# A fused attention and routing kernel: batch 1's queries projected sooner, the first quotient in halves, 1e-6 added by VectorE

## The chip, the cores and the metric

The kernel runs on one core of one Trainium2 chip. The metric is the device time of that core in microseconds (us). In what follows PE is TensorE, DVE is VectorE, ACT is ScalarE, POOL is GpSimd and SP is SyncE. All data are 32-bit floats. A "record" is a line of the profiler for one instruction; every matmul of this kernel leaves two of them.

## The reference

Two blocks follow each other. The first is a linear attention with a polynomial sketch: each query and key of 32 numbers is projected by two small matrices to 8 and 8 numbers, and their 64 products are its features. The second is a mixture of eight experts whose weights come from eight rounds of Sinkhorn normalization.

```python
batch, n_heads, seq, head_dim = (4, 4, 1088, 32);  r = 8

def phi(x):
    a = np.einsum('rd,bhsd->bhsr', S1, x)
    b = np.einsum('rd,bhsd->bhsr', S2, x)
    return np.einsum('bhsi,bhsj->bhsij', a, b).reshape(*x.shape[:-1], r * r)
q_p, k_p = (phi(q), phi(k))
kv = np.einsum('bhsf,bhsd->bhfd', k_p, v)
z = np.sum(k_p, axis=2)
num = np.einsum('bhsf,bhfd->bhsd', q_p, kv)
den = np.einsum('bhsf,bhf->bhs', q_p, z)[..., None] + 1e-06
attn = num / den                                  # x: (4352, 128) after a transpose

logits = x @ w_gate;  logits = logits - logits.max();  P = np.exp(logits)
for _ in range(8):
    P /= P.sum(1, keepdims=True) + 1e-09
    P /= P.sum(0, keepdims=True) + 1e-09
    P *= N / E
for e in range(E):                                # E = 8, F = 1024
    out += P[:, e:e + 1] * (np.maximum(x @ w1[e], 0.0) @ w2[e])
```

## The kernel before

The experts' matmuls are nearly all of the work. They are cut into *steps*: a step multiplies one tile of x by one 128-column piece of w1 (the line `first`, L914), ACT applies the relu, and the products with w2 (L1099) follow eight steps later. The products are computed by Strassen-like forms, for which DVE forms sums and differences of the relu's results (L931, later L978). The generator `work` yields one step at a time, and `fill(n)` puts steps worth `n` between the pieces of the attention and of the routing, so that PE has something to do while DVE, ACT and the transfers prepare the next piece.

```python
def fill(n):
    owed[0] += n
    while owed[0] > 0.25:
        owed[0] -= next(work)           # a step of 256 columns counts 0.57, of 480 columns 1
```

Batch 0 is the only one whose quotients can be had early. They are made in three chunks of queries, (0, 512), (512, 800) and (800, 1088). `fractions(c, 1)` puts the denominators of chunk c in a PSUM bank and `fractions(c, 0)` the numerators. `divide` turns them into x, transposed:

```python
def divide(c):
    lo, hi = chunks[c]
    n = hi - lo
    nb = n // 32
    pn, pd = (queries.pop((0, c, "pn", m)) for m in range(2))
    rd = wk.tile([P, 512], F32, tag="rd", name="rd")
    nc.vector.transpose(out=rd[:, 0:n], in_=pd[:, 0:n])
    rc = wk.tile([P, 16], F32, tag="rc", name="rc")[:, 0:nb]
    nc.vector.tensor_scalar_add(rc, rd[:, 0:n].rearrange("p (b r) -> p b r", r=32)[:, :, 0], 1e-6)
    nc.vector.reciprocal(rc, rc)
    rd = wk.tile([P, 512], F32, tag="rd", name="rd")
    nc.vector.transpose(out=rd[:, 0:n].rearrange("p (b r) -> p b r", r=32),
                        in_=rc.unsqueeze(2).to_broadcast([P, nb, 32]))
    nc.vector.tensor_tensor(xT[:, lo:hi], pn[:, 0:n], rd[:, 0:n], op=Alu.mult)
```

The other batches take another way. `queries_ab(b)` projects the queries (L426) and sends them through DRAM, so that they come back repeated in `ph` and `rb`; `times(b, c)` multiplies these to the features; `tops(b, c)` makes numerators and denominators of a third of the queries with tokens on the partitions, and adds 1e-6 to the denominators by a matmul of ones with a small constant; `over(b, c)` divides and transposes, and `take_over` brings the result into x through DRAM.

```python
eps = consts.tile([P, 3, H], F32, name="eps")
nc.gpsimd.memset(eps, 1e-6 / P)
# [...]
def tops(b, c):
    # [...] 12 matmuls of 66 columns into pn (L462)
    for s in range(2):
        nc.tensor.matmul(pn[64 * s:64 * (s + 1), :, :, D], ones[:, 0:64], eps, start=False, stop=True,
                         tile_position=(0, 64 * s))                                # L466
def over(b, c):
    pn = queries.pop((b, c))
    rc = wk.tile([P, 16], F32, tag="rc", name="rc")[:, 0:12].rearrange("p (t h) -> p t h", h=H)
    nc.vector.reciprocal(rc, pn[:, :, :, D])
    # [...] multiply, transpose
```

The first part of the program, where no step can be had before batch 0's first chunk is divided (the order of calls is the order on PE and DVE, but for what the scheduler moves within it):

```python
    for part_ in range(3):
        keys_products(0, part_)          # DVE, L331
    keys_sums(0)                         # PE, L347
    for i in range(2):
        multiply(0, i)                   # DVE, L384
    keys_kept(0)                         # ACT, L362: the sums, from PSUM into kvz
    transpose_q(1)                       # DVE, L297
    transpose_q(0, chunks[0][1])
    fractions(0, 1)                      # PE, L392: needs multiply(0) and kvz
    queries_ab(1)                        # PE, L426: needs transpose_q(1)
    fractions(0, 0)
    query_products(1)                    # PE, L376
    # [...] transfers of queries_ab(1)'s results
    divide(0)
    # [...]
    for i in range(2):
        multiply(1, i)
    transpose_k(1)
    fill(1.25)
    fractions(1, 1)
    fractions(1, 0)
    fill(0.75)
    divide(1)
    keys_ab(1)                           # PE, L314
```

Of the kernel before, what the change touches and what calls it, by code (L numbers as in the profile page):

```python
# [50 lines left out]
def kernel(  # L51
# [92 lines left out]
    for i in range(2):  # L144
        kvs.append(consts.tile([P, 2, 2, D + 1], F32, name=f"kvs{i}"))
        nc.gpsimd.memset(kvs[i], 0.0)

    eps = consts.tile([P, 3, H], F32, name="eps")
    nc.gpsimd.memset(eps, 1e-6 / P)

    v_slots = []
    for i in range(2):
# [142 lines left out]
    def transpose_q(b, lo=0, hi=S):  # L295
        to = kT if b == 1 else qT
        nc.vector.transpose(out=to[:, lo:hi], in_=loaded["q", b].rearrange("p a d -> p (a d)")[:, lo:hi])  # L297
# [94 lines left out]
            nc.tensor.matmul(t[64 * i:64 * (i + 1), 0:n], kvz[:, m, i].rearrange("p h d -> p (h d)"),  # L392
                             phs[0][:, i, lo:hi], start=True, stop=True, tile_position=(0, 64 * i))

    def divide(c):


        lo, hi = chunks[c]
        n = hi - lo
        nb = n // 32  # L400
        pn, pd = (queries.pop((0, c, "pn", m)) for m in range(2))
        rd = wk.tile([P, 512], F32, tag="rd", name="rd")
        nc.vector.transpose(out=rd[:, 0:n], in_=pd[:, 0:n])
        rc = wk.tile([P, 16], F32, tag="rc", name="rc")[:, 0:nb]
        nc.vector.tensor_scalar_add(rc, rd[:, 0:n].rearrange("p (b r) -> p b r", r=32)[:, :, 0], 1e-6)
        nc.vector.reciprocal(rc, rc)
        rd = wk.tile([P, 512], F32, tag="rd", name="rd")
        nc.vector.transpose(out=rd[:, 0:n].rearrange("p (b r) -> p b r", r=32),
                            in_=rc.unsqueeze(2).to_broadcast([P, nb, 32]))
        nc.vector.tensor_tensor(xT[:, lo:hi], pn[:, 0:n], rd[:, 0:n], op=Alu.mult)  # L410

# [41 lines left out]
    def tops(b, c):  # L455

        pn = bank()[:, 0:3 * H * (D + 1)].rearrange("p (t h d) -> p t h d", t=3, h=H)
        ph = third(phs[b % 2], c)
        for t in range(3):
            for i in range(2):  # L460
                for s in range(2):
                    nc.tensor.matmul(pn[64 * s:64 * (s + 1), t, 2 * i:2 * i + 2].rearrange("p h d -> p (h d)"),  # L462
                                     ph[:, i, s, 64 * t:64 * (t + 1)], kvs[b % 2][:, i].rearrange("p h d -> p (h d)"),
                                     start=(t == 0 and i == 0), stop=False, tile_position=(0, 64 * s))
        for s in range(2):
            nc.tensor.matmul(pn[64 * s:64 * (s + 1), :, :, D], ones[:, 0:64], eps, start=False, stop=True,  # L466
                             tile_position=(0, 64 * s))
        queries[b, c] = pn

    turned = {}  # L470
# [1 line left out]
    def over(b, c):  # L472
        pn = queries.pop((b, c))
        rc = wk.tile([P, 16], F32, tag="rc", name="rc")[:, 0:12].rearrange("p (t h) -> p t h", h=H)
        nc.vector.reciprocal(rc, pn[:, :, :, D])
        xs = wk.tile([P, 512], F32, tag="rd", name="rd")[:, 0:384].rearrange("p (h t d) -> p h t d", h=H, t=3)
        nc.vector.tensor_tensor(xs.rearrange("p h t d -> p t h d"), pn[:, :, :, 0:D],
                                rc.unsqueeze(3).to_broadcast([P, 3, H, D]), op=Alu.mult)
        if c == 0:
            turned[b] = wk.tile([P, H, W9], F32, tag="xt", name="xt", bufs=1)  # L480
        nc.vector.transpose(out=turned[b][:, :, 96 * c:96 * (c + 1)].rearrange("p h (t s) -> p h t s", t=3), in_=xs)
# [25 lines left out]
    def attention(b):  # L507


        follows = b + 1 < B  # L510
        keys_sums(b)
        times(b, 0)
        yield 2.2 if b == 1 else 2
        keys_kept(b)
        times(b, 1)
        tops(b, 0)
        if b == 1:
            transpose_q(2)
        yield 1.4
        times(b, 2)  # L520
        over(b, 0)
        tops(b, 1)
        if b == 1:
            queries_ab(2)
            repeat_a(2)
        if follows:
            repeat_b(b + 1)
        yield 1.4
        over(b, 1)
        if b + 1 == B:  # L530
            take_over(b, 0, 192, nc.gpsimd)
        yield 1.4
        tops(b, 2)
        if follows:
            transpose_k(b + 1)
        if b + 2 < B:
            load_k(b + 2)
            load_v(b + 2)
        yield 1.4
        over(b, 2)  # L540
        if b + 1 < B:
            take_over(b, 0, W9, nc.gpsimd)
        else:
            take_over(b, 192, W9, nc.sync)
        if follows:
            yield 0.7
            keys_ab(b + 1)
            yield 0.7
            if b == 1:
                transpose_q(3)  # L550
            keys_products(b + 1, 0)
            yield 1.4
            keys_products(b + 1, 1)
            if b == 1:
                queries_ab(3)
                repeat_a(3)
            yield 1.4
            keys_products(b + 1, 2)
            yield 1.4
# [10 lines left out]

    def routing():

        yield 5
        for c in range(len(chunks)):
            logits(c)
        yield 1
        for c in range(len(chunks)):
            logits_turned()
        lg = lgp[:, :, 0:E]
        mx = sk.tile([P, 1], F32, tag="mx", name="mx")  # L580
        nc.vector.tensor_reduce(out=mx, in_=lg, axis=AX.XY, op=Alu.max)
        yield 3
        pm = bank()[:, 0:P]
        for s in range(2):
            nc.tensor.matmul(pm[64 * s:64 * (s + 1)], mx.to_broadcast([P, 64]), ident, start=True, stop=True,
                             tile_position=(0, 64 * s))
        nc.vector.reduce_max(mx, pm, axis=AX.X)
        nc.vector.tensor_scalar(mx, mx, -1.0, 64 * math.log(2.0), op0=Alu.mult, op1=Alu.add)
        pw = p2s[0]
        nc.scalar.activation(out=pw[:, :, 0:E], in_=lg, func=Act.Exp, bias=mx[:, 0:1])  # L590

        step = 1.5 * 2.0 ** (23 - 149 + 64)
        nc.vector.tensor_scalar(pw[:, :, 0:E], pw[:, :, 0:E], step, step, op0=Alu.add, op1=Alu.subtract)
        for it in range(ITERS):
            rs = sk.tile([P, SA], F32, tag="rs", name="rs")
            nc.vector.reduce_sum(rs, pw, axis=AX.X)  # L596
            nc.vector.reciprocal(rs, rs)
            p1 = p1s[it % 2]
            nc.vector.scalar_tensor_tensor(p1[:, 0:SA], rs.unsqueeze(2).to_broadcast([P, SA, E]), UP,
                                           pw[:, :, 0:E], op0=Alu.mult, op1=Alu.mult)  # L600
            cs = sk.tile([P, E], F32, tag="cs", name="cs")
            nc.vector.reduce_sum(cs, p1.rearrange("p g e -> p e g"), axis=AX.X)  # L602
            yield 4.25
            pc = bank()[:, 0:E]
            for s in range(2):
                nc.tensor.matmul(pc[64 * s:64 * (s + 1)], ones[:, 0:64], cs, start=True, stop=True,
                                 tile_position=(0, 64 * s))
            cr = sk.tile([P, E], F32, tag="cr", name="cr")
            nc.vector.reciprocal(cr, pc)
            last = it == ITERS - 1  # L610
            pw = lgp if last else p2s[(it + 1) % 2]
            nc.vector.scalar_tensor_tensor(pw[:, :, 0:E], cr.unsqueeze(1).to_broadcast([P, SA, E]),
                                           float(N) / E * (1.0 if last else UP), p1[:, 0:SA],
                                           op0=Alu.mult, op1=Alu.mult)

        nc.vector.transpose(out=lgT.rearrange("p a s -> p (a s)"), in_=lgp.rearrange("p a e -> p (a e)"))
        for b in (1, 0, 2, 3):
            nc.sync.dma_start(out=pT[:, b * S:(b + 1) * S],
                                                  in_=lgT[32 * b:32 * b + E].rearrange("p a s -> p (a s)"))
# [300 lines left out]
    def two(k):  # L920
# [3 lines left out]
        h, ts, (later_h, earlier_h, t13) = hs[k] = room_of(k)  # L924

        def step(c):
            f, t = 2 * q + c // 2, c % 2
            first(k, f, t * n, (t + 1) * n, h[c], k % 2)

        def less(out, a, b):  # L930
            nc.vector.tensor_tensor(out, a, b, op=Alu.subtract)  # L931
# [242 lines left out]
# [3 lines that stand above are left out]
            owed[0] -= next(work)  # L1177

    with tc.manual_schedule(engines={engines.DVE, engines.PE, engines.Activation}):
# [7 lines left out]
        for part_ in range(3):  # L1187
            keys_products(0, part_)
        keys_sums(0)
        for i in range(2):  # L1190
            multiply(0, i)
        keys_kept(0)
        transpose_q(1)
        transpose_q(0, chunks[0][1])
        fractions(0, 1)
        queries_ab(1)
        fractions(0, 0)
        query_products(1)
        repeat_a(1)
        repeat_b(1)  # L1200
        divide(0)
        load_q(2)
    with tc.manual_schedule(engines={engines.DVE, engines.PE}):
        for i in range(2):
            multiply(1, i)
        transpose_k(1)
        load_k(2)
        fill(1.25)
        fractions(1, 1)
        fractions(1, 0)  # L1210
        fill(0.75)
        divide(1)
        keys_ab(1)
        fill(0.75)
# [56 lines left out]
```

## Time and profile before

| | |
|---|---|
| time, median of three runs | 920.4 us (920.19 to 921.06) |
| span of the profiled execution | 918.0 us |
| PE busy in matmuls | 911.2 us, 7442 records |
| L914, the first product, xe or xT by w1 | 569.8 + 119.7 us busy |
| L1099, the second product | 256.1 + 233.9 + 114.2 + 76.0 us busy |
| DVE busy | 678.9 us |
| ACT busy | 421.6 us |
| POOL busy | 204.0 us |
| granted clock of PE | full in every slice |

Busy times of PE's groups overlap, as two matmuls run at a time, one in each half of the array's columns; so PE's share of busy time doesn't tell how near PE is to what it can do. What a stage loses is read from the times at which matmuls start.

### The profile page before, as it was taken

What the parts mean: (1) busy time and instruction counts of PE and PEld (TensorE: products, weight loads), DVE (VectorE), ACT (ScalarE), POOL (GpSimd) and SP (SyncE); (2) the same over time, 40 slices, a digit from 0 to 9 for tenths busy, and PEclk for the clock granted to TensorE, in tenths of its full rate; (3) what the DMA queues carried; (4) which work ended last, traced back from release to release, by engine and by line L of the source; (5) the groups of instructions that cost most, each with busy time, mean ns of one, the idle gap of its engine ahead of it and who ended that gap; (6) DMA issues with size and microseconds to landing.
All of it is one profiled execution on the core that took longest, in us unless ns stands there. A gap on an engine that the chain in (4) does not pass through costs nothing.

```text
span 918.0 us, 18893 instructions
## 1 busy us (share of the span) xinstructions
PE 911.2 (99%) x7442; PEld 637.4 (69%) x7442; DVE 678.9 (74%) x1173; ACT 421.6 (46%) x915; POOL 204.0 (22%) x212
## 2 busy tenths in 40 slices
PE   9999999999999999999999999999999999999997
PEld 6777544466666677777777777777777655556886
DVE  7678699888776798666975656956567976758665
ACT  3455555554444454444544444544445444445443
POOL 3121100175545421201210010110100243210220
PEclk9999999999999999999999999999999999999999
DMA  9994100213454535534364343454445456453640
GB/s 254 308 273 163 54 1 1 70 64 127 148 150 139 186 119 174 165 110 150 114 185 134 117 143 112 132 187 127 133 122 165 130 170 195 162 166 92 177 153 13
DMA packets 91305, 128.15 MB, mean 140 GB/s; under 512 B 25392, under 2 KB 69504, under 8 KB 86480
## 3 DMA queue, kind: packets, MB, share of 16 engines
q1 hardware_dynamic: 88384, 121.42, 42.7%
q0 software_dynamic: 1600, 5.36, 2.1%
q8 instruction: 58, 0.95, 0.4%
q10 hardware_dynamic: 1232, 0.16, 0.1%
q14 instruction: 31, 0.25, 0.1%
HBM read 107.88 MB, written 19.05 MB: 138 GB/s over the span
## 4 chain that ended last, share of the span: by engine, by line
PE 97%; DVE 2%; ACT 1%; issue 0%; POOL 0%; DVEq 0%; POOLq 0%
PE a L914 51%; PE s L1099 41%; PE a L347 1%; PE a L462 1%; PE a L114 1%; DVE hb L931 1%; PE a L314 0%; PE s L376 0%; PE a L426 0%; PE s L392 0%; DVE cs L602 0%; PE a L496 0%; PE a L392 0%; ACT hb L918 0%; DVE rs L596 0%
## 5 line engine op out<-in xcount | busy, mean ns | idle before, releaser
L914 PE MATMUL a<-xe,w 128*64 128x256 f32 (+1 forms) x2560 | 569.8, 470 | 0.0
L918 ACT ACTIVATE hb<-a 128x256 f32<-128x256 f32 (+4 forms) x408 | 195.0, 480 | 241.5 <-PE a L914 209.3
L914 PEld LDWEIGHTS a<-xe,w 128*64 128x64 f32 x2560 | 263.0, 137 | 50.8 <-issue 1.8
L918 ACT ACTIVATE hx<-a 128x256 f32<-128x256 f32 (+1 forms) x360 | 167.3, 465 | 213.5 <-PE a L914 191.6
L1099 PE MATMUL s<-hb,ws 128*64 128x256 f32 (+3 forms) x1312 | 256.1, 395 | 0.2 <-DVE hb L931 0.2
L1099 PE MATMUL s<-hx,ws 128*64 128x256 f32 x1280 | 233.9, 379 | 0.0
L978 DVE TENSOR_TENSOR hb<-hb 128x512 f32<-128x512 f32 (+1 forms) x204 | 133.5, 664 | 102.8 <-ACT hb L918 98.8
L978 DVE TENSOR_TENSOR hx<-hx 128x512 f32<-128x512 f32 (+1 forms) x204 | 149.8, 744 | 65.0 <-ACT hx L918 60.2
L1099 PEld LDWEIGHTS s<-hb,ws 128*64 128x64 f32 x1312 | 134.9, 137 | 87.8 <-issue 64.5
L678 POOL TENSOR_TENSOR xe<-xT,xe 128x768 f32<-128x768 f32 (+2 forms) x41 | 80.3, 1958 | 481.2 <-DMA xe<-pT 377.0
L1099 PEld LDWEIGHTS s<-hx,ws 128*64 128x64 f32 x1280 | 132.7, 137 | 71.6 <-issue 50.3
L914 PE MATMUL a<-xT,w 128*64 128x416 f32 (+3 forms) x512 | 119.7, 462 | 0.0
L1099 PE MATMUL s<-hb,w 128*64 128x256 f32 (+3 forms) x536 | 114.2, 408 | 0.0
L1099 PE MATMUL s<-hx,w 128*64 128x256 f32 x384 | 76.0, 379 | 0.0
L931 DVE TENSOR_TENSOR hb<-hb 128x416 f32<-128x416 f32 (+7 forms) x84 | 60.7, 723 | 18.0 <-ACT hb L918 14.0
L1099 PEld LDWEIGHTS s<-hb,w 128*64 128x64 f32 x536 | 54.1, 137 | 19.0 <-issue 6.5
L914 PEld LDWEIGHTS a<-xT,w 128*64 128x64 f32 x512 | 48.9, 137 | 25.5 <-issue 15.7
L242 POOL TENSOR_TENSOR ws<-w 128x256 f32<-128x256 f32 (+1 forms) x70 | 60.5, 899 | 8.1 <-DMA w<-in_moe_w_dram 5.2
L931 DVE TENSOR_TENSOR hx<-hx 128x256 f32<-128x256 f32 (+1 forms) x65 | 39.5, 612 | 24.0 <-ACT hx L918 22.8
L1099 PEld LDWEIGHTS s<-hx,w 128*64 128x64 f32 x384 | 40.8, 137 | 6.6
L978 DVE TENSOR_TENSOR pqg<-hb 128x512 f32<-128x512 f32 x68 | 40.5, 637 | 0.0
L978 DVE TENSOR_TENSOR pqg<-hx 128x512 f32<-128x512 f32 x68 | 35.0, 554 | 0.0
(181 smaller groups left out, 485.0 us busy)
## 6 DMA issues: line engine op xcount, KB each, us to landing
w<-in_moe_w_dram SPq DMA_DIRECT2D x82, 512.0 KB, 5.5
ws<-ws SPq DMA_DIRECT2D x34, 1024.0 KB, 5.0
xe<-pT SPq DMA_DIRECT2D x34, 384.0 KB, 4.1
ws<-ws SPq DMA_DIRECT2D x12, 512.0 KB, 3.6
ph<-qa SPq DMA_DIRECT2D x12, 288.0 KB, 4.7
rb<-qb SPq DMA_DIRECT2D x3, 1152.0 KB, 7.2
pb<-pT SPq DMA_DIRECT2D x6, 384.0 KB, 8.3
kx<-in_k_dram SPq DMA_DIRECT2D x4, 544.0 KB, 4.0
```

The source lines that it names most:

```text
L114: nc.tensor.matmul(warm[:, 0:P], ones, ones, start=True, stop=True)
L242: tc.keep_in_program_order(nc.gpsimd.tensor_tensor(ws[:, c:c + len(ns)], blocks(x), blocks(y), op=Alu.subtract if off else Alu.add))
L347: nc.tensor.matmul(pv[64 * s:64 * (s + 1), i], kp[0:n, H * t + h].rearrange("p i j -> p (i j)"), vx[0:n, slots[h], t, :], start=(t == 0 an ...
L462: nc.tensor.matmul(pn[64 * s:64 * (s + 1), t, 2 * i:2 * i + 2].rearrange("p h d -> p (h d)"), ph[:, i, s, 64 * t:64 * (t + 1)], kvs[b % 2] ...
L678: tc.keep_in_program_order(nc.gpsimd.tensor_tensor(out, x, pb, op=Alu.mult))
L914: nc.tensor.matmul(ph[sl], loaded_w[j][0][:, P * f + H2 * s:P * f + H2 * (s + 1)], sources[j][:, lo:hi], start=True, stop=True, tile_posit ...
L918: nc.scalar.activation(out=out, in_=ph, func=Act.Relu)
L931: nc.vector.tensor_tensor(out, a, b, op=Alu.subtract)
L978: nc.vector.tensor_tensor(out if not isinstance(out, tuple) else places(*out), places(*a), places(*b) if isinstance(b, tuple) else b, op=A ...
L1099: nc.tensor.matmul(sums[g][i][H2 * s:H2 * (s + 1), n * place:n * (place + 1)], w, x, start=c == 1, stop=c == per, tile_position=(0, H2 * s))
```

## The change

It has five parts. (1) The queries of batch 1 are transposed and projected before `fractions(0, 1)`, where PE had waited for kvz. (2) The first quotient is made in two halves of 256 queries, and the first two blocks of steps are walked so that all four steps that need only the first 256 queries come first. (3) The 1e-6 of batches 1 to 3 is added by DVE and no longer by a matmul. (4) The larger piece of batch 3's x is sent by SP instead of POOL. (5) The numbers of steps ahead of numerators (`tops`), of fractions(1) and of the logits are larger, and some later ones smaller. The parts are meant to take waits and small matmuls off PE.

```diff
-    eps = consts.tile([P, 3, H], F32, name="eps")
-    nc.gpsimd.memset(eps, 1e-6 / P)
@@ divide
-    def divide(c):
+    def divide(c, parts=1):
-        n = hi - lo
+        n = (hi - lo) // parts
+        for i in range(0, hi - lo, n):
             # the same six operations, on pd[:, i:i + n], pn[:, i:i + n] and xT[:, lo + i:lo + i + n]
@@ tops
-                                     start=(t == 0 and i == 0), stop=False, tile_position=(0, 64 * s))
-        for s in range(2):
-            nc.tensor.matmul(pn[64 * s:64 * (s + 1), :, :, D], ones[:, 0:64], eps, start=False, stop=True,
-                             tile_position=(0, 64 * s))
+                                     start=(t == 0 and i == 0), stop=(t == 2 and i == 1), tile_position=(0, 64 * s))
@@ over
-        nc.vector.reciprocal(rc, pn[:, :, :, D])
+        nc.vector.tensor_scalar_add(rc, pn[:, :, :, D], 1e-6)
+        nc.vector.reciprocal(rc, rc)
@@ attention(b)
         keys_sums(b)
         times(b, 0)
-        yield 2.2 if b == 1 else 2
+        yield 2.8 if b == 1 else 2.5
         # [...]
         if b + 1 == B:
-            take_over(b, 0, 192, nc.gpsimd)
+            take_over(b, 0, 192, nc.sync)
         # [...]
-        yield 1.4
+        yield 1.4 if follows else 0.6
         over(b, 2)
@@ routing
-        yield 5
+        yield 6
         for c in range(len(chunks)):
             logits(c)
@@ two(k), the steps of a block of two tiles
         def step(c):
-            f, t = 2 * q + c // 2, c % 2
-            first(k, f, t * n, (t + 1) * n, h[c], k % 2)
+            b, f, t = k, c // 2, c % 2
+            if k < 2:
+                b, f, t = c // 2, c % 2, k
+            first(b, 2 * blocks[b][1] + f, t * n, (t + 1) * n, room_of(b)[0][2 * f + t], b % 2)
@@ the first part
         keys_sums(0)
+        transpose_q(1)
         for i in range(2):
             multiply(0, i)
         keys_kept(0)
-        transpose_q(1)
         transpose_q(0, chunks[0][1])
+        queries_ab(1)
         fractions(0, 1)
-        queries_ab(1)
         fractions(0, 0)
         query_products(1)
         # [...]
-        divide(0)
+        divide(0, 2)
         # [...]
-        fill(1.25)
+        fill(2.2)
         fractions(1, 1)
         fractions(1, 0)
-        fill(0.75)
+        fill(0.4)
         divide(1)
         keys_ab(1)
```

More of the change, by code (lines that the diff above doesn't have):

```diff
@@ L393, in fractions @@
                              phs[0][:, i, lo:hi], start=True, stop=True, tile_position=(0, 64 * i))
-    def divide(c):
+    def divide(c, parts=1):
         lo, hi = chunks[c]
-        n = hi - lo
+        n = (hi - lo) // parts
         nb = n // 32
         pn, pd = (queries.pop((0, c, "pn", m)) for m in range(2))
[L402 to L410, printed above, removed]
+        for i in range(0, hi - lo, n):
+            rd = wk.tile([P, 512], F32, tag="rd", name="rd")
+            nc.vector.transpose(out=rd[:, 0:n], in_=pd[:, i:i + n])
+            rc = wk.tile([P, 16], F32, tag="rc", name="rc")[:, 0:nb]
+            nc.vector.tensor_scalar_add(rc, rd[:, 0:n].rearrange("p (b r) -> p b r", r=32)[:, :, 0], 1e-6)
+            nc.vector.reciprocal(rc, rc)
+            rd = wk.tile([P, 512], F32, tag="rd", name="rd")
+            nc.vector.transpose(out=rd[:, 0:n].rearrange("p (b r) -> p b r", r=32),
+                                in_=rc.unsqueeze(2).to_broadcast([P, nb, 32]))
+            nc.vector.tensor_tensor(xT[:, lo + i:lo + i + n], pn[:, i:i + n], rd[:, 0:n], op=Alu.mult)
     def queries_ab(b):
@@ L474, in over @@
         rc = wk.tile([P, 16], F32, tag="rc", name="rc")[:, 0:12].rearrange("p (t h) -> p t h", h=H)
-        nc.vector.reciprocal(rc, pn[:, :, :, D])
+        nc.vector.tensor_scalar_add(rc, pn[:, :, :, D], 1e-6)
+        nc.vector.reciprocal(rc, rc)
         xs = wk.tile([P, 512], F32, tag="rd", name="rd")[:, 0:384].rearrange("p (h t d) -> p h t d", h=H, t=3)
```

## The prediction

> **What bounds the kernel now.** I read the page first, then the waits of PE, the chain, and the timeline of PE and DVE, stretch by stretch. The page:
>
> ```profile
> span 918.0 us, 18893 instructions
> ...
> PE 911.2 (99%) x7442; PEld 637.4 (69%) x7442; DVE 678.9 (74%) x1173; ACT 421.6 (46%) x915; POOL 204.0 (22%) x212
> ...
> PE 97%; DVE 2%; ACT 1%; issue 0%; POOL 0%; DVEq 0%; POOLq 0%
> ```
>
> PE carries the end: 97% of the chain. But busy time can't say how much is lost, so I counted columns. In the late, steady stage four steps with their products last 4.74 us by the chain; their columns at the rate of the timeline (two matmuls of 256 columns side by side every 0.43 us, which is 4 cycles of 2.4 GHz a column) come to 0.99 of that. Summed so over all 7442 records, the work is 890.1 us of the 918.0. Start times give where the other 28 lie: 4.4 us before 10 us (warm-up matmuls), 2.1 from 10 to 20, 5.9 from 20 to 100, 2.5 from 100 to 190, 7.7 spread evenly at 0.1 per 10 us, and 5.3 after the last matmul starts. The change touches only what lies from 10 to about 170 us, some 10 us of loss. That alone forbids a gain of 2% (18.4 us).
>
> The first part, on PE:
>
> ```profile
> 10.30 2.46 PE L347 MATMUL a<-v,kp 128*64 128x64 f32 x72
> 13.39 1.08 PE L392 MATMUL a<-ph,kvz 128*64 128x512 f32 x4 [0.63 <-ACT kvz L362]
> 14.30 1.15 PE L426 MATMUL a<-kT,wdq 128*64 128x192 f32 x12
> 15.28 1.03 PE L392 MATMUL a<-ph,kvz 128*64 128x512 f32 x4
> 16.24 1.24 PE L376 MATMUL s<-qT,wq 64*128 64x288 f32 x8
> 17.41 1.08 PE L914 MATMUL a<-xT,w 128*64 128x256 f32 x8
> 18.45 1.19 PE L392 MATMUL s<-ph,kvz 128*64 128x288 f32 x8
> 19.47 1.03 PE L914 MATMUL a<-xT,w 128*64 128x256 f32 x8
> 20.34 1.10 PE L314 MATMUL a<-wd,kT 128*64 128x64 f32 x32
> ```
>
> (start, duration, engine, line, out<-in, and in brackets an idle time and who ended it). There is one open wait, 0.63 us on ACT's copy to kvz. Some 0.1 us each is lost at 14.30, 17.41 (on the quotient) and 18.45 (on multiply(1)). DVE beside it:
>
> ```profile
> 12.14 1.30 DVE L297 STREAM_TRANSPOSE kT<-qx 128x1088 f32<-128x1088 f32 x1
> 13.36 0.73 DVE L297 STREAM_TRANSPOSE qT<-qx 128x576 f32<-128x576 f32 x1
> 14.55 0.72 DVE L403 STREAM_TRANSPOSE rd<-a 128x512 f32<-128x512 f32 x1 [0.46 <-PE a L392]
> ...
> 16.61 0.69 DVE L410 TENSOR_TENSOR xT<-a,rd 128x512 f32<-128x512 f32 x1
> 17.58 0.82 DVE L384 TENSOR_TENSOR ph<-ph,s 128x288 f32<-128x288 f32 x2 [0.28 <-PE s L376]
> ```
>
> DVE is never idle for long here: a divide of 512 lasts 2.75 us (14.55 to 17.30) and feeds PE at once. The small matmul that adds 1e-6, and a place in the routing where DVE's order costs PE time:
>
> ```profile
> 34.04 0.87 PE L462 MATMUL a<-kvs,ph 128*64 128x66 f32 x24
> 34.74 0.24 PE L466 MATMUL a<-eps,ones 128*64 128x12 f32 x4
> 34.83 0.63 PE L914 MATMUL a<-xT,w 128*64 128x256 f32 x4
> ```
>
> ```profile
> 161.82 0.95 DVE L931 TENSOR_TENSOR hb<-hb 128x768 f32<-128x768 f32 x1
> 162.69 0.20 DVE L609 RECIPROCAL cr<-a 128x8 f32<-128x8 f32 x1
> ...
> 164.79 0.66 DVE L602 TENSOR_REDUCE cs<-p 128x8 f32<-128x280 f32 x1
> 165.37 1.14 DVE L931 TENSOR_TENSOR hb<-hb 128x384 f32<-128x384 f32 x2
> ```
>
> **What the Trainium skill says.** "Perfetto Trace Analysis", section "Identifying the Most-Contended Engine", warns that the busy share of matmuls doesn't measure how near TensorE is to its limit; so it is here: 99% busy, 890 of 918 us of work. "TensorE: Matmul & The Clock Gate", "Back-to-back issue gap", gives matmuls of 1 to 64 columns a floor of about 60 cycles (25 ns): L466's four records of 12 columns occupy 34.74 to 34.83, 22 ns each, where their columns alone are worth 5. "VectorE: DVE Perf Modes", "The TRN2 errata", says that each instruction pays a fixed latency beside its elements: the transpose takes 0.72 us for 512 columns and 0.44 to 0.48 for 288 (L403 at 19.60 and 26.20), so a divide in halves costs more than one whole. "DMA: Bandwidth & Descriptors", "Issuing engines are not separate DMA queues", says that issuing from another engine saves only the issue: I expect nothing of part 4 by itself.
>
> **Part 3, 1e-6 by DVE.** Nine pairs of matmuls go (three batches by three thirds). Each occupies 0.087 us between the starts at 34.74 and 34.83; the other places give 0.06 to 0.09. 9 x 0.087 = 0.78 us, all on PE, which has no wait there: a gain of 0.75. DVE gets nine additions of 12 columns; the like of it (L405) lasts 0.17 and begins the next 0.21 later: 1.9 us of DVE between 36 and 100 us, where DVE idles 4.6 us before 32.8, 2.1 before 41.5 and 2.7 before 86.7. Off the path.
>
> **Parts 1 and 2, the first 25 us.** I lay the new order on the old durations. DVE: transpose of q(1) 10.94 to 12.24 (its load lands at 10.67, just in time), multiply(0) 12.16 to 13.43, transpose of q(0) to 14.09. PE: L347 is followed at 12.67 by queries_ab(1), 0.98 us, to 13.65; kvz is ready at 13.34, multiply(0) at 13.43, so the 0.63 wait is gone. Fractions(0, 1) to 14.52, fractions(0, 0) to 15.40, query_products(1) to 16.45. DVE begins to divide 1.16 after fractions(0, 1) begins, as before: 14.81. Half of it takes 0.46 + 0.21 + 0.26 + 0.52 + 0.42 = 1.87 (transpose, addition, reciprocal, transpose, product, by the spacing of the 288 chunk at 19.60, scaled to 256): 16.68, and PE starts steps at 16.78, after 0.33 of waiting. Four steps of 0.43 end at 18.51. The second half and multiply(1), which the built order interleaves, keep DVE until 18.7 (multiply(1)) and 19.05 (the last product); fractions(1) start at 18.74, a wait of 0.23, and end at 19.72; a fifth step to 20.16; keys_ab(1) waits 0.1 for transpose_k(1), 20.27. Before, keys_ab(1) began at 20.34 with four steps done. So the new order is ahead by a step, 0.43, and 0.07: 0.5 us. Of the 0.63 and the small losses a good half stays; DVE takes the rest. Queries of batch 1 leave 1.5 us sooner, and rb, which lands at 32.66 and is used at 32.79, comes sooner too; but PE did not wait for it.
>
> **Part 5, more steps ahead.** Before the numerators of the later batches PE loses a little, some 0.1 to 0.3 us at 62.6, 70.4, 87.4 and 96 by the start times, about 1 us together, part of it the change of shape that stays. I credit 0.2. The routing moves by three steps against the main work, so its DVE chains of 2.7 us (L609 to L602) fall elsewhere between the sums L931. Before, three of eight chains cut such a group in two, as above at 162.69 (others at 136.3 and 142.2), and PE waited at 139.64 (0.22), 145.51 (0.14) and 165.97 (0.35). In the built order of the changed kernel only two cuts by a chain remain, one at the maximum and exp (3.6 us long, with about 5.5 us until its sums are needed) and one at the last transpose (2.0 us). I credit 0.3 of the 0.7.
>
> **The sum.** 0.75 + 0.5 + 0.2 + 0.3 = 1.75 us. 920.4 - 1.75 = 918.65; I say 918.7.
>
> **The rivals.** (a) The routing ends too late. Counted in columns along the built order, its last sums stand at 156.5 us of work instead of 153.2, 3.3 later, while the first weighted step stands 1.4 later. Before, POOL began to weigh x at 179.98, when the transfer landed at 179.47; the first 512 columns of 768, two thirds of 3.02 us, are done at 182.0, and PE uses them at 184.21: 2.2 us to spare. The net delay is 3.3 - 1.4 = 1.9. That speaks for just no wait; and w2's load, which SP now issues ahead of the routing's result, must wait for PE's last product with the old w2, due at about 171.5, while the result is due at 172.8. If it fails, PE loses 0.5 to 1.5 us there: 919.5 to 920. (b) DVE becomes the bound of the first part: halves cost it 1 us more than one divide of 512, and if these durations are 0.1 longer each the four steps only fill a longer wait. The gain of 0.5 becomes 0: 919.2. (c) The waits only move: DVE's backlog in the routing lets PE wait at other sums. Then 0.3 turns into -0.7: 919.7. (d) All waits before numerators and in the routing go: another 1.2, 917.5. (e) Batch 3's x comes later, because SP issues the second piece's first transfer ahead of the first piece's loads. Landing at about 105.5, it is 3 us ahead of the logits, which move to about 108.5; a wait is unlikely.
>
> **Range and chances.** The parts are uncertain by 0.1, 0.4, 0.3 and 0.7, rival (a) adds up to 1, and the median by 0.3: 917.4 to 920.1 holds it 8 times in 10. All rivals together stay within 2 us, 2% is 18: same 0.98, faster 0.01, slower 0.01.
>
> **What would show it.** The idle time before L392 by kvz gone, and keys_ab(1) near 20.3 with five steps ahead of it; a wait of 0.2 to 0.4 before the first step, and one before fractions(1). No matmul of 12 columns, nine additions before the reciprocals, and PE straight from the numerators to the next step. POOL's first weighing no later than 182, no idle PE near 184, and fewer gaps before L1099 from 135 to 170. A stretch of PE idle over 1 us at 184, or transposes of 256 over 0.5 us, would make the prediction wrong.

## The result, and the profile after

The changed kernel takes 923.43 us (median; 922.18 to 924.35), the kernel before 920.39 (920.18 to 921.06): 1.003 times, 95% interval 1.0017 to 1.0043. The prediction said 918.7, 917.4 to 920.1. The change makes the kernel slower by about 3 us where a gain of 1.75 was forecast. The page of the changed kernel:

```profile
span 922.2 us, 18837 instructions
...
PE 910.9 (99%) x7406; PEld 566.3 (61%) x7406; DVE 694.0 (75%) x1187; ACT 420.4 (46%) x915; POOL 207.6 (23%) x206
...
PE 89%; DMA 5%; DVE 2%; POOL 2%; ACT 1%; issue 0%; SPq 0%; POOLq 0%; DVEq 0%; ACTq 0%
```

PE is as busy as before (910.9 for 911.2 us), with 18 matmuls (36 records) fewer. What tells more is the chain of work that ends last: PE holds 89% of it instead of 97%, and transfers (5%) and POOL (2%) have come in. It spends some 70 us more outside PE than before, 46 us of this between 240 and 320 us, where it goes round a loop of POOL and transfers. The waits of PE in the changed kernel (who was waited for, us in total, times, longest) show where it stands:

```profile
PE a L910 <- POOL xe L674: 1.5, 3, 0.5
PE a L424 <- DVE qT L294: 1.5, 1, 1.5
...
PE a L910 <- DVE rd L473: 0.6, 2, 0.3
PE a L460 <- DVE ph L451: 0.6, 1, 0.6
```

Before, this view named only the set-up wait for `own` (1.0), the 0.6 on kvz and a 0.2 in the routing. The 0.6 is gone, as predicted. New are the four shown, 0.5 for batch 1's keys, and two of 0.2.

The loss of PE, counted as in the prediction (start time less the columns' work of all records so far), in us by stretches of the span. E6 is an experiment below, the changed kernel without its attention yields:

| stretch, us | before | after | after less before | E6 |
|---|---|---|---|---|
| to 50 | 8.59 | 8.06 | -0.53 | 7.69 |
| 50 to 80 | 2.03 | 4.73 | +2.70 | 3.08 |
| 80 to 120 | 2.10 | 2.88 | +0.78 | 1.84 |
| 120 to 170 | 2.11 | 1.26 | -0.85 | 1.23 |
| 170 to 280 | 0.95 | 1.30 | +0.35 | 0.95 |
| 280 to 340 | 0.98 | 2.69 | +1.71 | 0.57 |
| 340 to 910 | 5.79 | 5.76 | -0.03 | 6.16 |

The stretches in which the prediction saw gains (the first 50 us, the routing from 120 to 170) did gain, 1.4 us together. Two stretches in which it expected next to nothing took 4.4: 50 to 80 and 280 to 340. (The two profiled executions are 4.2 us apart, spans of 922.2 and 918.0, where the medians are 3.0 apart; the table divides up the 4.2.)

**The wait at 54 us.** The changed kernel's timeline, PE, DVE and POOL, around the projection of batch 3's queries (start, duration, engine, line; idle time and its releaser in brackets):

```profile
50.27 2.90 DVE L930 TENSOR_TENSOR hb<-hb 128x576 f32<-128x576 f32 x1 [0.73 <-ACT hb L914]
50.45 0.74 POOL L201 TENSOR_TENSOR ws<-ws,w 128x256 f32<-128x256 f32 x1
...
51.83 0.72 POOL L203 TENSOR_TENSOR ws<-w,ws 128x256 f32<-128x256 f32 x1
53.10 1.30 DVE L294 STREAM_TRANSPOSE qT<-qx 128x1088 f32<-128x1088 f32 x1
54.54 0.87 PE L424 MATMUL a<-qT,wdq 128*64 128x192 f32 x8 [1.47 <-DVE qT L294]
```

One DVE sum that elsewhere takes 0.75 us lasts 2.90: it stands through POOL's three sums of weights. The transpose of the queries is behind it in DVE's queue, and PE waits 1.47 us for it. POOL's sums begin only now because POOL's queue is in order and its transfer of batch 1's x (L482) waits for that batch's last quotient; with more steps put ahead, the quotient ends at 49.5. Before, it ended at 45.9:

```profile
45.97 3.73 DVE L931 TENSOR_TENSOR hb<-hb 128x576 f32<-128x576 f32 x3
...
49.62 1.30 DVE L297 STREAM_TRANSPOSE qT<-qx 128x1088 f32<-128x1088 f32 x1
...
51.09 0.54 PE L426 MATMUL a<-qT,wdq 128*64 128x192 f32 x2
```

The same collision was there (three sums in 3.73 us), but the transpose ended at 50.92 and PE came for it at 51.09, 0.17 us later. The change brought no new collision. It used up 0.17 us of room.

**The waits from 68 to 73 us.** DVE's part of the changed kernel's timeline, with PE's waits:

```profile
64.49 0.46 DVE L737 TENSOR_TENSOR z<-x,z 128x288 f32<-128x288 f32 x1 [2.47 <-ACT x L746]
...
67.43 0.69 DVE L930 TENSOR_TENSOR hb<-hb 128x512 f32<-128x512 f32 x1 [1.31 <-ACT hb L914]
68.72 0.96 DVE L451 TENSOR_TENSOR ph<-ph,rb 128x768 f32<-128x768 f32 x1
69.82 0.92 PE L460 MATMUL a<-kvs,ph 128*64 128x66 f32 x24 [0.58 <-DVE ph L451]
```

DVE idles 2.47 us, 0.72 (between the lines) and 1.31 here and still makes PE wait. The profile shows nothing that the product `ph*rb` waits for itself, but it stands behind three operations of steps that were put ahead of it and that wait for ACT. Idle time in an in-order queue isn't room for what stands behind. The quotient that follows late, at 71.6, keeps a PSUM bank until its product `rd` is done, and PE waits 0.27 for that bank at 72.70, and 0.34 for another at 80.87.

**The waits from 282 to 322 us.** Here PE works through the experts in items. For each item POOL weighs x, that is, multiplies it by the tokens' routing weights (L674). POOL and the transfer queue of SP, in the changed kernel:

```profile
280.06 2.29 POOL L674 TENSOR_TENSOR xe<-xT,xe 128x768 f32<-128x768 f32 x1 [7.12 <-DMA xe<-pT]
...
292.19 0.33 SPq L243 DMA_DIRECT2D ws<-ws  x1
292.61 0.38 SPq L670 DMA_DIRECT2D xe<-pT  x1
299.75 2.28 POOL L674 TENSOR_TENSOR xe<-xT,xe 128x768 f32<-128x768 f32 x1 [7.59 <-DMA xe<-pT]
```

POOL weighs x, sums the weights of the next item (283.01 to 292.2), and SP stores these sums (L243). The next routing row (L670) stands behind that store in SP's queue, lands 7 us later, and only then can POOL weigh again. The loop takes 19.69 us here (280.06 to 299.75). Where PE waits for nothing, it needs 18.95 us for an item (before, four items from 222.31 to 298.12 us). Its 19.68 in the changed kernel (282.41 to 302.09) are the loop's pace, with half a us of waiting in each item.

The loop isn't always so slow. Its rounds from 241.64 us on last 19.07, 19.35, 19.69 and 19.74 us, those of E6 from 255.78 on 19.07, 19.00 and 18.57. In the rounds of 19.7 us POOL's own work has grown. In the changed kernel the weighing above, at 280.06, falls on sums of DVE that begin at the same time:

```profile
279.99 0.69 DVE L977 TENSOR_TENSOR hb<-hb 128x512 f32<-128x512 f32 x1 [2.31 <-ACT hb L914]
280.60 2.64 DVE L977 TENSOR_TENSOR pqg<-hb 128x512 f32<-128x512 f32 x2
```

In E6 it falls into the idle time of DVE ahead of the same sums:

```profile
274.85 1.82 POOL L674 TENSOR_TENSOR xe<-xT,xe 128x768 f32<-128x768 f32 x1 [7.41 <-DMA xe<-pT]
276.88 0.69 DVE L977 TENSOR_TENSOR hb<-hb 128x512 f32<-128x512 f32 x1 [2.31 <-ACT hb L914]
277.49 1.56 DVE L977 TENSOR_TENSOR pqg<-hb 128x512 f32<-128x512 f32 x2
```

The weighing takes 2.29 us for 1.82, and the ten sums of weights after it 9.15 for 8.57. Two things come together, then, and no run separates them: the loop has no room left (0.05 us from the end of a weighing to PE's use of it at 243.51; 1.09 before and 0.90 in E6 at the same item), and its own operations are longer. Little room alone doesn't make the loss. E10 below has 0.08 us of room at that item, but its next two rounds last 18.64 and 18.76 us, with sums of 8.95 and 8.76 us and a weighing of 1.82, and no such wait follows. Nor does the late first weighing by itself: it is at 184.64, 4.66 us later than before (179.98), but PE's first use of it is 3.87 us later as well (188.08 for 184.21).

### The profile page after: what moved, and what is told of

The parts are those of the page before. It is cut to its first block, busy times and chain, and to the rows that moved or that the text cites. A ratio compares the mean times of both kernels' runs of the same rounds, so it can differ in the third digit from the quotient of the medians.

```text
span 922.2 us, 18837 instructions
## 1 busy us (share of the span) xinstructions
PE 910.9 (99%) x7406; PEld 566.3 (61%) x7406; DVE 694.0 (75%) x1187; ACT 420.4 (46%) x915; POOL 207.6 (23%) x206
## 4 chain that ended last, share of the span: by engine, by line
PE 89%; DMA 5%; DVE 2%; POOL 2%; ACT 1%; issue 0%; SPq 0%; POOLq 0%; DVEq 0%; ACTq 0%
PE a L910 48%; PE s L1098 40%; DMA xe<-pT 2%; DMA kx<-in_k_dram 1%; POOL ws L239 1%; DMA w<-in_moe_w_dram 1%; DVE hb L930 1%; POOL xe L674 1%; PE a L344 1%; DMA v<-in_v_dram 1%; PE a L460 0%; DVE kT L299 0%; PE a L424 0%; PE a L311 0%; DVE ph L451 0%
## 5 line engine op out<-in xcount | busy, mean ns | idle before, releaser
L910 PE MATMUL a<-xe,w 128*64 128x256 f32 (+1 forms) x2560 | 532.5, 470 | 1.5 <-POOL xe L674 1.5
L910 PEld LDWEIGHTS a<-xe,w 128*64 128x64 f32 x2560 | 214.8, 137 | 86.2 <-POOL xe L674 2.9
L1098 PE MATMUL s<-hb,ws 128*64 128x256 f32 (+3 forms) x1312 | 237.9, 395 | 0.0
L1098 PE MATMUL s<-hx,ws 128*64 128x256 f32 x1280 | 213.6, 379 | 0.0
L977 DVE TENSOR_TENSOR hx<-hx 128x512 f32<-128x512 f32 (+1 forms) x204 | 156.2, 777 | 54.4 <-ACT hx L914 48.8
L674 POOL TENSOR_TENSOR xe<-xT,xe 128x768 f32<-128x768 f32 (+2 forms) x41 | 83.6, 2041 | 501.2 <-DMA xe<-pT 356.6
L1098 PEld LDWEIGHTS s<-hb,ws 128*64 128x64 f32 x1312 | 113.0, 137 | 101.0 <-issue 68.4
L1098 PEld LDWEIGHTS s<-hx,ws 128*64 128x64 f32 x1280 | 109.9, 137 | 93.1 <-issue 67.1
L1098 PE MATMUL s<-hb,w 128*64 128x256 f32 (+3 forms) x536 | 108.1, 408 | 0.0
L1098 PE MATMUL s<-hx,w 128*64 128x256 f32 x384 | 70.6, 379 | 0.0
L977 DVE TENSOR_TENSOR pqg<-hb 128x512 f32<-128x512 f32 x68 | 48.4, 752 | 0.0
```

The costliest lines, as they stand in the source:

```text
L674: tc.keep_in_program_order(nc.gpsimd.tensor_tensor(out, x, pb, op=Alu.mult))
L910: nc.tensor.matmul(ph[sl], loaded_w[j][0][:, P * f + H2 * s:P * f + H2 * (s + 1)], sources[j][:, lo:hi], start=True, stop=True, tile_posit ...
L977: nc.vector.tensor_tensor(out if not isinstance(out, tuple) else places(*out), places(*a), places(*b) if isinstance(b, tuple) else b, op=A ...
L1098: nc.tensor.matmul(sums[g][i][H2 * s:H2 * (s + 1), n * place:n * (place + 1)], w, x, start=c == 1, stop=c == per, tile_position=(0, H2 * s))
```

## Experiments on the change: undone, and each part alone

Times are medians with the ratio to the kernel before on the same chip (there 920.04 to 920.36 us) and its 95% interval. In the texts on record, theory A says that the added steps make the loss, B the first 25 us, C the 1e-6 on VectorE. Where the text subtracts the medians of two experiments, these can come from different chips. By the ratios, the change costs 2.8 us instead of 3.04, E1 gives back 2.3, E6 3.7 and E7 1.9 us, and E9 to E12 lie 1.7, 1.1, 1.5 and 0.6 us above E6: differences of a few tenths shouldn't be read.

**E1: all added steps taken back** from the changed kernel.

```diff
-        yield 2.8 if b == 1 else 2.5
+        yield 2.2 if b == 1 else 2
-        yield 1.4 if follows else 0.6
+        yield 1.4
-        yield 6      # routing
+        yield 5
```

> The changed kernel with the numbers of steps ahead of numerators, of the last quotient and of the logits as before (2.2 and 2, 1.4, 5); the rest of the change stays. Theory A, more steps ahead: they put sums that wait for later matmuls in front of batch b's products and quotients in DVE's queue, and start the routing, and with it POOL, later. Then the waits at 54.5 (1.5 us), 70 to 81 (1.2) and 282, 302, 322 (0.5 each) go, and the time is 918.5 to 919.5. Theory B, the first part (parts 1 and 2) shifts the phase of the steps: nothing comes back, 922 to 924. Theory C, the nine additions lengthen each quotient on DVE: also 922 to 924.

920.68 us, ratio 1.0005 (0.9996 to 1.0013): 2.75 us of the 3.04 come back, and none of the waits at 54, 68 to 73 and 282 to 322 us stands in its trace. Theory A, though 1.2 us above the upper end of what it expected.

**E2: only the added steps**, on the kernel before (the same three lines, the other way).

> The kernel before with only the larger numbers of steps ahead (2.8 and 2.5, 0.6 at the end of batch 3, 6 before the logits). Theory A: most of the loss is here, 923 to 925, with PE waiting for DVE at 54 and at 70 and for POOL near 280 to 320. Theories B and C: 920 to 921.

922.77 us, 1.0028 (1.0018 to 1.0039). A again, 0.2 below its range. Its trace has waits for the weighed tokens, 2.1 us in three at 261 to 320 us, but neither the one at 54 nor those at 68 to 73, which A had expected. So the added steps bring POOL's waits by themselves, and DVE's waits only together with the rest of the change; with which part of it wasn't separated.

**E3: only the first 25 us** (the new order, the halves, the fills), on the kernel before.

> The kernel before with only parts 1 and 2, the first 25 us (order, quotient in halves, walk of the first two blocks, fills of 2.2 and 0.4). Theory A: a gain of 0.4, 920.0. Theory B: the loss is here, 922 to 923, with the wait at 54 for DVE.

920.21 us, 1.0001 (0.9992 to 1.0009). Against B; of the predicted 0.5 nothing can be measured. The trace gives it and takes it: the loss at 24 us is 0.2 us lower than before, and at 35.5 PE waits 0.6 us for the first numerators, whose `rb` comes too late.

**E4: only the 1e-6 on VectorE**, on the kernel before.

> The kernel before with only part 3, 1e-6 added by DVE instead of by a matmul. Theory A: a gain of 0.75, 919.6. Theory C: the longer quotients make PE wait for banks and products, 921.5 to 923.

922.07 us, 1.0017 (1.0009 to 1.0025). A miss for A: this part alone is slower, within C's range. Of the waits that C names, the trace has one for a bank, 0.3 us. It puts most of the loss in another place, the logits:

```profile
108.08 1.26 PE L491 MATMUL a<-xT,wg 128*32 128x512 f32 x15 [0.97 <-DMA xT<-xd]
```

PE waits 0.97 us for batch 3's x, which goes through DRAM. In the kernel before, the second piece's store was issued at 98.58 and the read at 101.19; here 99.44 and 104.12. So 0.86 us of the delay is the quotient's, and 2.1 are the store's own time, which was 2.6 us before and 4.7 here. Whether each execution has that longer store is open: there is one trace.

## Experiments on the cause: which step, through which queue

**E5: only the routing's start back** (`yield 5`), in the changed kernel.

> The changed kernel with only the routing's head start put back from 6 steps to 5. Theory P (the three waits of 0.56 us for weighed tokens at 282 to 322 us stand because the routing ends later and GpSimd's loop, whose period is one item of work, never makes up for it): the waits there vanish, 1.7 us come back, and of the routing's small waits between 140 and 170 us about 1 us returns; 922.3 us (921.6 to 923.0). Rival Q (those waits come of slower GpSimd operations, not of a late start): they stay, and the time is 923.4 or above.

921.77 us, 1.0018 (1.001 to 1.0026). The first weighing moves from 184.64 to 182.40, the three POOL waits are gone, and the wait at 54 us is 1.5 us still. The 1.7 us come back as theory P says; the small waits of the routing, which it expected to return, do not. But POOL's operations are short again as well (weighings of 1.82 us from 258 us on, sums of 8.4 to 8.9), so this run doesn't rule out rival Q, that slower GpSimd operations make the waits.

**E6: only the attention's steps back** (the first two lines of E1), routing left at 6.

> The changed kernel with only the attention's head starts put back (2.2 and 2 steps for 2.8 and 2.5, and 1.4 for 0.6), the routing left at 6. Theory A (more steps put ahead on VectorE fill its queue, so that its products and transposes come late): the waits at 54, 70, 73 and 81 us go, 3.3 us; if the waits at 282 to 322 us stay, 920.1 us, and if they go as well, 918.5 us. Rival Q (a wait given up in one place is taken in another): at least half of it comes back before 120 us, 921.8 us or more.

919.08 us, 0.999 (0.9983 to 0.9997): faster than both kernels, 4.35 us below the changed one. In its waits nothing is left but the set-up's 1.0 us and one of 0.3 for a sum at 69.9 us, and the page's chain is PE's again:

```profile
PE 98%; DVE 1%; ACT 0%; issue 0%; POOL 0%; DVEq 0%; ACTq 0%; POOLq 0%
```

The POOL waits went too, although the routing still starts after 6 steps. The attention ends sooner; the first weighing (179.93) and PE's first use of it (182.98) come some 5 us sooner. Both new groups of waits hang on the attention's yields. Rival Q fails: its loss at 120 us is 12.61, the changed kernel's 15.67.

**E7: batch 3's queries transposed sooner.** The changed kernel, all yields as in the change:

```diff
         over(b, 2)
+        if b == 1:
+            transpose_q(3)
...
-            if b == 1:
-                transpose_q(3)
             keys_products(b + 1, 0)
```

> The changed kernel with batch 3's queries transposed right after batch 1's last quotient, ahead of the step's sums, so that GpSimd's sums no longer stand between. Theory A1 (the wait of 1.5 us at 54 us is one VectorE sum stretched from 0.75 to 2.90 us while GpSimd adds, with the transpose queued behind it): the wait goes and nothing else moves, 921.8 us (921.2 to 922.4). Rival Q (the delay only passes to the next reader of VectorE's results within 20 us): 923.0 us or more, with a new wait between 54 and 75 us.

920.88 us, 1.0009 (1.0002 to 1.0016). One line moved gives back 2.5 us. In its trace the sum is stretched all the same (POOL adds from 50.07 to 52.17), but nothing that PE needs soon stands behind it:

```profile
49.08 1.27 DVE L294 STREAM_TRANSPOSE qT<-qx 128x1088 f32<-128x1088 f32 x1
...
50.28 2.52 DVE L930 TENSOR_TENSOR hb<-hb 128x576 f32<-128x576 f32 x1
```

A1 holds for the wait: it is gone, and the ones at 67.8, 70.6 and 78.8 us keep their 0.59, 0.26 and 0.34. The rest of the gain I had not expected: the POOL waits vanish too. The first weighing is 2.28 us sooner (182.36), but PE's first use of it is 2.06 us sooner as well (186.02), so the loop has won little on PE: 0.40 us of room at 241.4 instead of 0.05. From 258 us on its weighings take 1.82 us again. The two losses don't add, but neither is simply the cause of the other: E2 has POOL's waits without the wait at 54 us, and E5 the wait at 54 us without POOL's.

**E8: the loop opened.** The changed kernel, with the store out of SP's queue:

```diff
-        nc.sync.dma_start(out=stored_four[e], in_=ws)
+        nc.gpsimd.dma_start(out=stored_four[e], in_=ws)
```

> The changed kernel with the sums of four blocks stored through GpSimd's own queue instead of SyncE's, so that SyncE's next load of a routing row no longer stands behind that store. Theory P (GpSimd's loop of load, weighing, sums and store is closed through SyncE's queue, and its period of 19.7 us is above the item's 19.0): the loop opens, the three waits at 282 to 322 us vanish, 921.7 us (921.2 to 922.3). Rival Q (GpSimd waits for a buffer that TensorE frees, or for the landing alone): the waits stay, 923.4 us.

921.70 us, 1.0031 (1.0016 to 1.0046). Five runs, two of them at 923.8 and 924.7, so that median and ratio differ and the gain is uncertain; the trace is clear. The waits at 282 to 322 us are gone, and the loss at 340 us is 18.66 for 20.92. Its trace:

```profile
276.66 7.99 POOL L239 TENSOR_TENSOR ws<-w 128x256 f32<-128x256 f32 x10 [8.01 <-PE a L910]
281.47 0.33 SPq L670 DMA_DIRECT2D xe<-pT  x1
...
285.56 1.83 POOL L674 TENSOR_TENSOR xe<-xT,xe 128x768 f32<-128x768 f32 x1
```

The row is fetched while POOL still sums (281.47), the weighing follows the sums with no idle time, and from 243 us on it is done 10 to 13 us ahead of PE. The first weighing was as late as in the changed kernel (184.5): with the loop open the late start brings no wait for POOL, and theory P holds against the Q of this run (a buffer, or the landing alone).

## Experiments on what each part is worth without the bad yields

All four are compared with E6 (919.08 us, ratio 0.999). They ran on another chip, where the kernel before takes 920.04 us instead of 920.29; measured from it, the differences from E6 are 0.25 us larger than those of the medians.

**E9: E6 with the last quotient after 0.6 steps again** (the changed kernel with only the first yield put back).

> The changed kernel with only the first of the two attention yields put back (2.2 and 2 steps for 2.8 and 2.5); the last quotient of batch 3 still comes after 0.6 steps. Theory A (the added steps ahead of the first numerators, in batches 1 and 2, make all the waits between 54 and 81 us): none of them stands, and the time is that of the kernel with both put back, 919.1 us (918.6 to 919.7). Rival R (the shortened last quotient carries part of the loss, by the wait of 0.37 us at 116 us and what follows it): 919.8 us or more.

921.01 us, 1.0009 (1.0001 to 1.0016): 1.9 us more than E6. Of the changed kernel's waits between 54 and 81 us none stands in its trace, and none for POOL: as theory A says, it is the yield ahead of the first numerators that makes them. The time is rival R's, but not by the wait at 116 us that I named, which isn't there. The trace has two other places:

```profile
108.19 0.67 PEld L492 LDWEIGHTS a<-xT,wg 128*32 128x32 f32 x15 [0.68 <-DMA xT<-xd]
161.39 0.54 PE L1098 MATMUL s<-hb,ws 128*64 128x384 f32 x1 [0.43 <-DVE hb L930]
```

Six routing steps count from the attention's end; ending it 0.8 steps sooner puts the logits at 107.36 instead of 108.61, and they meet the landing of batch 3's x. E1 has 5 steps after 1.4, one routing step fewer, and waits in the same two places (0.63 at 108.3, 0.62 of loss at 161.6) at 920.68. E1 less E6 is what the sixth step buys, 1.6 us; E9 less E6 is what the shortened yield costs, 1.9: one cancels the other.

**E10: E6 with the matrix products for the 1e-6 again.**

> The kernel with both attention yields put back, and besides with the 1e-6 added by the matrix products on TensorE again. By the prediction's step (24 small products gone are worth 0.75 us when no wait takes their place) it is 0.75 us slower than with them gone: 919.8 us. Rival C (VectorE's longer quotient costs as much as TensorE saves, as the part alone on the kernel before had it, 1.7 us slower): it is equal or faster, 919.1 us or less.

919.69 us, 1.0002 (0.9993 to 1.0011): 0.6 us slower by the medians, the intervals overlap. (The 24 products of the text are 18, in 36 records.) It agrees with the predicted 0.75, but it isn't clean: in its trace `rb` lands about 1.1 us later than in E6 (its product starts at 34.18 for 33.10), and PE waits 0.89 us there.

**E11: E6 with the first 25 us as before.**

> The kernel with both attention yields put back, and besides with the first 25 us as before (batch 1's queries after the products, the first quotient whole, the old order of steps and fills). By the prediction's step the first part is worth 0.5 us: 919.6 us. Rival C (worth nothing, as alone on the kernel before, or passed on to the wait for batch 1's keys at 20 us): 919.1 us.

920.74 us, 1.0006 (0.9998 to 1.0014): 1.7 us slower by the medians, where 0.5 was expected. At 50 us its loss is 1.03 us above E6's (8.72 for 7.69); the 0.63 for kvz is back among it. Another 0.61 stands at 160.7 us, where PE waits for a sum that DVE has late.

**E12: E6 with batch 3's first piece sent by GpSimd again.**

> The kernel with both attention yields put back, and besides with the first two thirds of batch 3's x sent by GpSimd again and not by SyncE. By the prediction's step this moves no wait by itself: 919.1 us. Rival S (the landing of batch 3's x is what the logits wait for, as in the kernel with the 1e-6 alone, where TensorE stood 1.25 us for it at 108 us): a wait of the logits for that transfer of 0.5 to 1.5 us stands near 107 us, 919.6 to 920.6 us.

919.53 us, 0.9996 (0.9988 to 1.0003), the profiled span 916.7 for 917.0. It can't be told from E6, and no wait for the transfer stands near the logits: rival S fails here.

## Why the prediction was wrong, point by point

- **The step that failed: "Part 5, more steps ahead", and in it "I credit 0.2"** for the later numerators. I asked only which small waits of PE more steps could fill. The steps also put their sums into DVE's queue ahead of what PE needs next, and I laid out DVE's queue for the first 25 us and for the routing but never for 44 to 81 us. Measured: the attention's yields cost 4.35 us (the changed kernel less E6; 3.7 by the ratios) in place of the gain of 0.2, and the whole of part 5 alone costs 2.4 us (E2) in place of the 0.5 credited. By E9 it is the yield of 2.8 and 2.5 steps that makes the waits. A line would have warned me: the queries' transpose at 49.62 to 50.92 and PE's use at 51.09 left 0.17 us.
- **Rival (a), the routing ends too late**, was the right rival in the wrong place. I computed a net delay of 1.9 us against 2.2 to spare at the first weighing, and it was right that PE shows no idle time at 184. Measured, the first 512 columns are done at 186.27 for 181.60 and PE uses them at 188.08 for 184.21, a net delay of 0.8 us. What I left out is POOL's loop after it: I never set the loop's period beside PE's 18.95 us for an item, nor asked what its operations do when they fall on DVE's. The bill came at 282 us. (The rival's own sum is off too: 918.7 with 0.5 to 1.5 us added is 919.2 to 920.2.)
- **The routing, "I credit 0.3"**: right in sign and too small. From 120 to 170 us the loss falls by 0.85 us, in E6 as well (0.88). E1 against E6 puts the sixth step at a gain of 1.6 us, logits included; with the attention's yields in place the same step costs 1.7 us (the changed kernel against E5), by POOL's waits.
- **Parts 1 and 2, 0.5**: the mechanism came as laid out, to 0.3 us (fractions done at 15.25 for 15.40, steps from 16.50 for 16.78, batch 1's keys at 20.44 for 20.27). From the timeline of the changed kernel, PE:

```profile
13.31 2.01 PE L389 MATMUL a<-ph,kvz 128*64 128x512 f32 x8
...
16.50 1.95 PE L910 MATMUL a<-xT,w 128*64 128x256 f32 x16
...
20.44 0.77 PE L311 MATMUL a<-wd,kT 128*64 128x64 f32 x19 [0.54 <-DVE kT L301]
```

  The fractions start with no idle time before them: the kvz wait is gone. A wait of 0.54 us for batch 1's transposed keys has come, because DVE starts on them 0.49 us late (their load lands later). That `rb` comes sooner, though PE doesn't wait for it, failed too: it was in use at 32.79 before, at 33.91 in the changed kernel, at 33.10 in E6 and at 34.45 in E3, although PE projects the queries sooner. Two of the four transfers of `qb` leave sooner than before (14.89 us for 16.85, by POOL), the other two later (19.04 for 18.20, by SP), and the read into `rb` is issued when it was before (25.45 for 25.43). The first part is worth nothing measurable alone (E3) and 1.7 us with the rest in place (E11): the same part differs by more than its predicted size, by what stands behind it.
- **Part 3, 0.75**: the matmuls and the additions are as counted (0.17 us each), and with the yields mended it is worth 0.6, not separated from zero. Alone it costs 1.7 us (E4), and in its trace 1.25 us of loss stand where the logits meet batch 3's x, which comes later; this is an interaction with the routing's start that I looked for only in rival (e).
- **Part 4, nothing**: so it is (E12).
- **The range** allowed 1 us for rival (a) and 0.7 for part 5 to the bad side. Nothing in it stood for DVE's queue from 44 to 81 us or for POOL's loop from 240 us on.

What stays open: how the added steps take the loop's room, and how much of POOL's waits is the lost room and how much the longer operations; why the store of batch 3's x takes 4.7 us in one trace and 2.6 in another, so how much of E4's loss each execution has; and how much of part 3's 0.6 us is `rb`'s landing, which moves by itself.

## What to carry to other kernels

Before you put more work ahead of a stage in an in-order queue, list what stands behind it in that queue and how many tenths of a microsecond each of these has until its reader comes; an engine that idles may still be the one that is late. For a loop over several engines and queues, compare its period with that of what it feeds, taken where this doesn't wait (here 18.95 us; while it waits it shows the loop's own 19.68). If the two are nearly equal, a few tenths in one link decide between catching up and a wait in every round, far from the cause; the cure is to take one link (here a store ahead of a load in one queue) out of the loop. Parts of a change that move the same queues don't add: measure each in the company in which it is to stay.

## What the runs showed of the hardware

- A VectorE sum of two SBUF operands stands still while GpSimd adds: 2.90 us for 0.75 beside three GpSimd additions of 2.1 us in all (2.90 in E5 and E8 too, 2.52 in E7). A transpose isn't held: in E6 it lasts 1.30 us beside these additions (48.35 to 49.65, with GpSimd adding from 48.51), in E7 1.27 with GpSimd adding nothing. "SBUF — State Buffer" of the Trainium skill, section "SBUF: two separate sides", says that a VectorE operation with two SBUF inputs and a GpSimd operation that reads SBUF lock each other out: the one that starts first keeps the lock for its whole instruction. The trace agrees on the operands. It differs in the order: the VectorE instruction was held through three GpSimd instructions in a row, although by the records it had started 0.18 us before the first of them.
- The same weighing of 768 columns on GpSimd took 2.29 us in the changed kernel and 1.82 in E6 (at 280 and 275 us), the ten sums after it 9.15 and 8.57. In the changed kernel it ran beside two-input sums of VectorE, in E6 beside none, as the lines above show. That it is the same lock, from the other side, is likely and wasn't tested.
- Transfers through DRAM come at times that differ from trace to trace. `rb` was in use at 33.10 us in E6 and at 30.84 in E12, kernels that differ only from some 90 us on. A store to DRAM that is read back at once took 2.6 to 4.7 us from its issue to the issue of the read, with the same bytes and queue.
